# Six of nine token blocks taken as three pairs, gate and value from seven products of sums of quarters

## The chip, the core and the metric

The kernel runs on one core of a Trainium2 chip. The metric is device time in microseconds (us). Of the core's engines, TensorE (PE) multiplies matrices into banks of PSUM, VectorE (DVE) and ScalarE (ACT) do elementwise work, and SyncE (SP) issues most DMAs.

## The reference

Attention in chunks of 64 tokens, then a feed-forward layer with a gate. B = H = 8, S = 576, D = 64, all in float32:

```python
scores = scale * np.matmul(q_c, k_c.transpose(0, 1, 2, 4, 3))   # per chunk of 64
scores = scores - np.max(scores, axis=-1, keepdims=True)
attn = np.exp(scores)
attn = attn / (np.sum(attn, axis=-1, keepdims=True) + 1e-09)
out = np.matmul(attn, v_c)
...
x = np.ascontiguousarray(attn_out.transpose(0, 2, 1, 3)).reshape(B * S, H * D)   # 4608 x 512
g = x @ w_gate                                                   # 512 x 1536
silu = g * (1.0 / (1.0 + np.exp(-g)))
val = x @ w_val
return (silu * val @ w_out)                                      # 1536 x 512
```

## The kernel before

The 4608 tokens are 9 blocks of 512 (4 tiles of 128). A float32 operand is split into an upper and a lower half (`split`: a cast on ACT, a subtraction on DVE), and a product is three matmuls: lower by upper, upper by lower, upper by upper. The hidden dimension of 1536 is taken in 12 steps `f` of 128. In each step the gate and the value of a block are 12 matmuls each, of 128x128 by 128x512 (4 slices of the 512 inputs by 3), into a bank of `ps_gv`, which has two (line 416). `silu` on ACT reads the gate's bank, `times` on DVE multiplies by the value's bank, `parts` splits the result h into hh (ACT) and hl (DVE), and `project` does 12 matmuls against the step's output weights into four banks that stay open over the 12 steps (lines 460 to 462). `lag` issues the projection one step late.

The work runs in stages:

- an opening, written out as a string of operations: attention of blocks 0 and 1, and step 0;
- a **weight loop** over f = 1 to 10. The weights come as pairs of 32-bit words and are put together by `Up` (gate and value weights of step f + 1) and `Out` (output weights of step f) with scale, shift, below, power, weigh and join; then `upper` and `lower` make the halves `w` (128 x 2 x 1024). Each pass does gate and value of blocks 0 and 1 and the projection of block 0. The h of block 1 is written to DRAM (`put_off`);
- step 11, then a **late loop**: 12 projections of block 1, from h read back (`prepare`), beside block 2's softmax;
- blocks 2 to 8 one by one (`block`). Beside the steps of a block the next one's attention is done (`scores` behind step 1, `exponents` in step 3, `normalize`, `turn`, `values`, `ready`).

The order on PE, ACT and DVE is that in which the code is written, and on SP too up to `loading.__exit__` (line 746); behind it SP's order is chosen by the framework. All weights stay on chip, tiles `w0` to `w11` and `wo0` to `wo11`; out weights are split anew in each block (`out_weights`, pool `wp` of two buffers). Softmax of a block sits in `s_sb`, what `turn` makes of it in `turned`, and x in `xh0`, `xl0`, `xh1`, `xl1`.

## Time and profile before

| | |
|---|---|
| three runs | 952.35 us median (951.77 to 952.48) |
| the profiled execution | 952.15 us, of which the profile's span is 950.4 |
| instructions in it | 14625 |
| granted TensorE clock, mean | 1.0 |
| DMA | 63.85 MB, 67 GB/s mean; 50.33 MB read from and 12.58 MB written to device memory |
| DMAs of `raw<-in_wgv` (SP), 1024 KB | 11, 7.0 us median from issue to landing |
| DMAs of `out<-o_sb` (SP), 256 KB | 35, 2.3 us |
| DMAs of `h<-h` (ACT), 256 KB | 12, 2.0 us |
| DMAs of `h_in<-h` (SP), 512 KB | 6, 3.5 us |

A row of a group reads: line, engine, operation, written tile and read tile, shape, count, then busy time in all, mean of one in ns, the engine's idle time just ahead of these instructions, and what ended it. A row of the timeline reads: start and length in us, engine, line, operation, tiles, shapes, count, and in square brackets the wait ahead of it and who ended it. A row of who waited for whom ends with the wait in all, the count and the longest. A row of the windows has the stretch, then for each engine its busy share with the count of instructions, the granted clock, the DMA engines' busy share and the rate in GB/s.

### The profile page before, as it was taken

Reading aid. Unit: us, or ns where it says so; the run is one execution under the profiler, and the core shown is the slowest. Engines: PE = TensorE matmul, PEld = TensorE weight load, DVE = VectorE, ACT = ScalarE, POOL = GpSimd, SP = SyncE. Lnnn points to the kernel's source line nnn. Section 1 sums busy time; section 2 is a strip of 40 time slices with the busy share of each in tenths; the row PEclk is TensorE's granted clock in tenths of the full one; section 3 lists DMA queues with packets and bytes.
Section 4 is the critical chain, followed back from the end, with each engine's and each line's share of the span. In section 5 each row is a group of like instructions: output and inputs, shape, how many; then the busy total and the mean of one; then the engine's idle time right before and its main releaser. Section 6 shows DMA issues by size and latency. Waiting matters only on the chain.

```text
span 950.4 us, 14625 instructions
## 1 busy us (share of the span) xinstructions
PE 940.5 (99%) x6299; PEld 778.6 (82%) x6299; DVE 480.4 (51%) x792; ACT 336.3 (35%) x540; POOL 7.0 (1%) x14
## 2 busy tenths in 40 slices
PE   7999999999999999999999999999999999999998
PEld 6888888888888888888888888888888888888886
DVE  7966666574475336632574337533663256432222
ACT  4745444354332333133323233233423342332222
POOL 1100000000000000000000000000000000000000
PEclk9999999999999999999999999999999999999999
DMA  9614332443300230022102030023002210000001
GB/s 363 228 54 155 155 111 99 156 167 112 89 1 1 89 87 3 1 90 67 23 0 90 1 90 1 5 84 90 1 1 89 67 23 1 1 16 29 1 1 44
DMA packets 43936, 63.85 MB, mean 67 GB/s; under 512 B 27488, under 2 KB 27744, under 8 KB 42464
## 3 DMA queue, kind: packets, MB, share of 16 engines
q1 hardware_dynamic: 42144, 59.78, 18.3%
q10 hardware_dynamic: 1728, 3.15, 0.9%
q8 instruction: 49, 0.80, 0.3%
q14 instruction: 15, 0.12, 0.0%
HBM read 50.33 MB, written 12.58 MB: 66 GB/s over the span
## 4 chain that ended last, share of the span: by engine, by line
PE 97%; DMA 2%; SPq 0%; issue 0%; ACT 0%; DVE 0%
PE ps_gv L416 62%; PE ps_o L460 10%; PE ps_o L462 10%; PE ps_o L461 10%; PE ps_a L228 2%; DMA qk_t<-in_qk 2%; PE ps_a L306 1%; PE ps_a L406 1%; PE ps_a L585 0%; PE ps_a L392 0%; DMA out<-o_sb 0%; PE pt L392 0%; SPq L200 0%; SPq L154 0%; SPq L345 0%
## 5 line engine op out<-in xcount | busy, mean ns | idle before, releaser
L416 PE MATMUL ps_gv<-xh,w 128*128 128x512 f32 x1728 | 531.0, 389 | 0.0
L416 PEld LDWEIGHTS ps_gv<-xh,w 128*128 128x128 f32 x1728 | 324.3, 188 | 67.4 <-ACT xh L535 0.2
L416 PE MATMUL ps_gv<-xl,w 128*128 128x512 f32 x864 | 336.1, 391 | 0.0
L441 DVE SCALAR_TENSOR_TENSOR h<-ps_gv,h 128x512 f32<-128x512 f32 x108 | 74.6, 691 | 365.1 <-PE ps_gv L416 357.8
L416 PEld LDWEIGHTS ps_gv<-xl,w 128*128 128x128 f32 x864 | 162.1, 188 | 34.6 <-issue 0.4
L434 ACT ACTIVATE h<-ps_gv 128x512 f32<-128x512 f32 x108 | 64.6, 598 | 313.0 <-PE ps_gv L416 313.0
L460 PE MATMUL ps_o<-woh,hl 128*128 128x512 f32 x432 | 168.4, 390 | 0.0
L461 PE MATMUL ps_o<-wol,hh 128*128 128x512 f32 x432 | 168.1, 389 | 0.0
L462 PE MATMUL ps_o<-woh,hh 128*128 128x512 f32 x432 | 168.1, 389 | 0.0
L64 ACT CAST hh<-h 128x512 fp32r<-128x512 f32 x96 | 59.6, 620 | 182.7 <-DVE h L441 182.7
L461 PEld LDWEIGHTS ps_o<-wol,hh 128*128 128x128 f32 x432 | 81.1, 188 | 16.9
L460 PEld LDWEIGHTS ps_o<-woh,hl 128*128 128x128 f32 x432 | 81.1, 188 | 16.9
L462 PEld LDWEIGHTS ps_o<-woh,hh 128*128 128x128 f32 x432 | 81.1, 188 | 16.8
L293 DVE STREAM_TRANSPOSE turned<-s_sb 32x256 f32<-32x256 f32 x192 | 83.7, 436 | 2.7
L65 DVE TENSOR_TENSOR wol<-wo,woh 128x512 fp32r<-128x512 f32 x108 | 73.8, 684 | 12.7 <-ACT woh L64 12.6
L65 DVE TENSOR_TENSOR hl<-h,hh 128x512 fp32r<-128x512 f32 x96 | 66.4, 692 | 18.1 <-ACT hh L64 11.1
L64 ACT CAST woh<-wo 128x512 fp32r<-128x512 f32 x108 | 66.1, 612 | 15.9 <-DVE wo L102 15.9
L228 PEld LDWEIGHTS ps_a<-qk_t 64*64 64x64 f32 x1152 | 18.0, 135 | 5.4 <-issue 3.4
L228 PE MATMUL ps_a<-qk_t 64*64 64x64 f32 x1152 | 19.8, 220 | 1.6 <-DMA qk_t<-in_qk 1.6
L99 DVE TENSOR_TENSOR t<-t 128x1024 bf16<-128x1024 bf16 (+1 forms) x13 | 8.5, 650 | 22.1 <-ACT t L91 21.9
L475 ACT ACTIVATE o_sb<-ps_o 128x512 f32<-128x512 f32 (+1 forms) x36 | 18.6, 593 | 2.2 <-PE ps_o L462 2.0
L136 ACT CAST w<-t 128x1024 fp32r<-128x1024 f32 x11 | 11.6, 1054 | 16.7 <-DVE t L102 16.7
(70 smaller groups left out, 409.1 us busy)
## 6 DMA issues: line engine op xcount, KB each, us to landing
raw<-in_wgv SPq DMA_DIRECT2D x11, 1024.0 KB, 7.0
qk_t<-in_qk SPq DMA_DIRECT2D x10, 1024.0 KB, 7.5
out<-o_sb SPq DMA_DIRECT2D x35, 256.0 KB, 2.3
qk_t<-in_qk SPq DMA_DIRECT2D x16, 512.0 KB, 4.0
raw<-in_wo SPq DMA_DIRECT2D x6, 1024.0 KB, 4.9
v_t<-in_v SPq DMA_DIRECT2D x28, 128.0 KB, 2.7
h<-h ACTq DMA_DIRECT2D x12, 256.0 KB, 2.0
h_in<-h SPq DMA_DIRECT2D x6, 512.0 KB, 3.5
```

The source lines that it names most:

```text
L64: nc.scalar.copy(out=hi, in_=src)
L65: (engine or nc.vector).tensor_tensor(out=lo, in0=src, in1=hi.bitcast(F32), op=ALU.subtract)
L136: nc.scalar.copy(out=self.w[:, 0], in_=self.t)
L228: nc.tensor.matmul(ps[h][j * C:(j + 1) * C, i, u // 2, :], part[:, us:us + C], part[:, M * P + us:M * P + us + C], start=not more or first ...
L293: nc.vector.transpose(out=self.turned[to:to + 32, p:p + 2, j, :, 32 * (i % 2):32 * (i % 2) + 32], in_=src[32 * i:32 * i + 32, :, o // 2, 3 ...
L416: nc.tensor.matmul(ps, w, x, start=first and (k, i) == which[0], stop=last and (k, i) == which[-1])
L434: nc.scalar.activation(h, pg, AF.Silu, scale=2.0 ** -8)
L441: nc.vector.scalar_tensor_tensor(out=h, in0=pv, scalar=2.0 ** -8, in1=h, op0=ALU.mult, op1=ALU.mult)
L460: nc.tensor.matmul(o, hl[:, ts], woh, start=f == 0, stop=False)
L461: nc.tensor.matmul(o, hh[:, ts], wol, start=False, stop=False)
L462: nc.tensor.matmul(o, hh[:, ts], woh, start=False, stop=f == NF - 1)
L475: nc.scalar.activation(o_sb[:, m], o[:, m], AF.Copy, scale=2.0 ** -8)
```

## The change

Blocks 3 to 8 are taken as pairs (3, 4), (5, 6) and (7, 8). A pair's x is a 2 x 2 matrix of quarters (block by half of the 512 inputs), and so is a step's weight (half of the inputs by gate or value). `gated_pair` makes gate and value of both blocks from seven products of 6 matmuls (`seventh`), of quarters and of sums of quarters (`FACTORS`, `x0` to `x6`), in place of 4 x 12 matmuls. Three products are copied out of PSUM by ACT and three are added to by DVE. The projection of the first block lags as before, but a tile of it is put between the products (`turn_of`); the second block's h is kept on chip in the tiles of `xh0` to `xl1`, and its 12 projections follow in `second_steps`.

The factors on the weights' side (`w`, and the sums of its quarters, `ts`, split into `th` by `Quarters`) are not all kept on chip. In the weight loop each pass adds three subtractions, a cast and a subtraction for the sums and saves them to DRAM (`save`); steps 0 and 1, which the loop doesn't reach, are caught up by `redo` in block 2. The halves `w` are saved in block 2 (`save_w`), the split output weights in the weight loop (`save_o`). From then on they are loaded: 1024 KB of `w` and 1024 KB of sums per step of a pair (`load_weights`, two steps ahead, two buffers of each), and 512 KB of output weights per projection (`out_again`, three buffers), from block 1's late projections on. The output weights' raw tiles become four in turn. While block 2 runs alone, the attention of blocks 3 and 4 is done beside it, with its order by step in `behind`; later pairs' attention lies beside the steps of the pair ahead (`behind`, `later`).

```diff
-    wp = ctx.enter_context(tc.tile_pool(name="wp", bufs=2))
+    wp = ctx.enter_context(tc.tile_pool(name="wp", bufs=3))
...
+    Q = NK // 2 * P
+    class Quarters:
+        def __init__(self, f):
+            self.f = f
+        def again(self):
+            self.both = const.tile([P, 2, 4 * Q], F32, name="th", tag="th")
+            w = w_both[self.f].bitcast(F32)
+            nc.vector.tensor_tensor(out=self.both[:, 0], in0=w[:, 0], in1=w[:, 1], op=ALU.add)
+            return self.both[:, 0]
+        def sums(self, t):
+            self.s = s = const.tile([P, 4, Q], F32, name="ts", tag="ts")
+            t = t.rearrange("p (i q) -> p i q", q=Q)
+            nc.vector.tensor_tensor(out=s[:, 0:2], in0=t[:, 2:4], in1=t[:, 0:3:2], op=ALU.subtract)
+            nc.vector.tensor_tensor(out=s[:, 2], in0=t[:, 3], in1=s[:, 0], op=ALU.subtract)
+            nc.vector.tensor_tensor(out=s[:, 3], in0=t[:, 1], in1=s[:, 2], op=ALU.subtract)
+        def upper(self):
+            self.halves = const.tile([P, 2, 4 * Q], F32R, name="th", tag="th")
+            self.s = self.s.rearrange("p i q -> p (i q)")
+            nc.scalar.copy(out=self.halves[:, 0], in_=self.s)
+        def lower(self):
+            nc.vector.tensor_tensor(out=self.halves[:, 1], in0=self.s, in1=self.halves[:, 0].bitcast(F32), op=ALU.subtract)
+        def save(self):
+            kept_t[self.f] = store.tile([P, 2, 4 * Q], F32, name=f"t{self.f}")
+            nc.sync.dma_start(out=kept_t[self.f], in_=self.halves.bitcast(F32))
+    kept_w, kept_t, kept_o = {}, {}, {}
+    def save_w(f):
+        kept_w[f] = store.tile([P, 2, 4 * Q], F32, name=f"w{f}")
+        nc.sync.dma_start(out=kept_w[f], in_=w_both[f].bitcast(F32))
...
-            wo_raw.append(const.tile([P, DM], F32, name=f"wo{self.f}"))
+            wo_raw.append(const.tile([P, DM], F32, name="wo", tag=f"wo{self.f % 4}"))
...
-    def out_weights(f, engine=None):
-        woh = wp.tile([P, DM], F32R, name="woh")
-        wol = wp.tile([P, DM], F32R, name="wol")
-        split(wo_raw[f], woh, wol, engine)
-        return woh, wol
+    def out_weights(f):
+        both = wp.tile([P, 2, DM], F32R, name="both", tag="wo")
+        split(wo_raw[f], both[:, 0], both[:, 1])
+        kept_o[f] = store.tile([P, 2, DM], F32, name=f"o{f}")
+        out_now[f] = both
+        return both[:, 0], both[:, 1]
...
+    out_now = {}
+    def save_o(f):
+        nc.sync.dma_start(out=kept_o[f], in_=out_now[f].bitcast(F32))
+    def out_again(f):
+        both = wp.tile([P, 2, DM], F32R, name="both", tag="wo")
+        nc.sync.dma_start(out=both.bitcast(F32), in_=kept_o[f])
...
+    quarters = None
     for f in range(1, NF - 1):
         w, o = up[f + 1], down[f]
         if f + 2 < NF:
             up[f + 2].load()
+        save_o(f - 1)
         down[f + 1].load()
+        if quarters:
+            quarters.save()
+        quarters = Quarters(f + 1)
         h0 = gate(a0, f)
...
         w.lower()
+        quarters.sums(w.t)
         o.weigh()
         o.join()
         if f + 2 < NF:
             up[f + 2].scale()
         down[f + 1].scale()
+        quarters.upper()
         wo_f = out_weights(f)
         lag(p0, wo_f)
+        quarters.lower()
         h1 = gate(a1, f)
         pv1 = value(a1, f)
...
-        return p, out_weights(f)
+        return p, out_again(f)
...
     put.append(prepare(1))
+    save_o(f - 1)
+    quarters.save()
+    save_o(f)
     pv1 = value(a1, f)
     times(h1, pv1)
     put_off(h1)
...
+    class Pair:
+        def __init__(self, b, turned):
+            self.a = [Attn(b)]
+            self.b, self.turned, self.x = b + 1, turned, {}
+        def second(self):
+            self.a.append(Attn(self.b, const, "th", self.turned))
+            return self.a[1]
+        def quarter(self, i, j):
+            return self.a[i].s[:, 2 * j:2 * j + 2].rearrange("p n c h k -> p (n c h k)")
+        def halves(self, i, src):
+            x = self.x[i] = const.tile([P, 2, NK // 2, N], F32R, name="x", tag=f"w{i}")
+            split(src, *(x[:, j].rearrange("p k n -> p (k n)") for j in range(2)))
+        def x0(self):
+            self.halves(0, self.quarter(0, 0))
+        def x1(self):
+            self.sum = ld.tile([P, NK // 2 * N], F32, name="sum", tag="qk_t")
+            nc.vector.tensor_tensor(out=self.sum, in0=self.quarter(1, 0), in1=self.quarter(1, 1), op=ALU.add)
+            self.halves(1, self.sum)
+        def x2(self):
+            a11, a21 = self.quarter(0, 0), self.quarter(1, 0)
+            nc.vector.tensor_tensor(out=a21, in0=a11, in1=a21, op=ALU.subtract)
+            nc.vector.tensor_tensor(out=a11, in0=self.sum, in1=a11, op=ALU.subtract)
+            self.halves(2, a11)
+        def x3(self):
+            self.halves(3, self.quarter(0, 1))
+        def x4(self):
+            self.halves(4, self.quarter(1, 0))
+        def x5(self):
+            a11, a12 = self.quarter(0, 0), self.quarter(0, 1)
+            nc.vector.tensor_tensor(out=a12, in0=a12, in1=a11, op=ALU.subtract)
+            self.halves(5, a12)
+        def x6(self):
+            self.halves(6, self.quarter(1, 1))
...
+    FACTORS = (0, 0), (1, 0), (1, 2), (0, 1), (1, 1), (0, 3), (1, 3)
+    loaded = {}
+    def load_weights(f):
+        tags = ("w7", "w8") if f % 2 == 0 else ("w9", "w10")
+        loaded[f] = []
+        for kept, tag in zip((kept_w, kept_t), tags):
+            t = const.tile([P, 2, 4 * Q], F32R, name="factors", tag=tag)
+            nc.sync.dma_start(out=t.bitcast(F32), in_=kept[f])
+            loaded[f].append(t)
+    def seventh(ps, pair, f, i, first):
+        which, q = FACTORS[i]
+        w = loaded[f][which].rearrange("p h (i k m) -> p h i k m", i=4, m=P)[:, :, q]
+        x = pair.x[i]
+        for k in range(NK // 2):
+            for n, (u, v) in enumerate(((0, 1), (1, 0), (0, 0))):
+                nc.tensor.matmul(ps, w[:, u, k], x[:, v, k], start=first and k == 0 and n == 0,
+                                 stop=k == NK // 2 - 1 and n == 2, skip_group_check=True)
...
+        ps1 = ps_a.tile([P, N], F32, name="ps_a", tag="ps_a")
+        ps2 = ps_gv.tile([P, N], F32, name="ps_gv")
+        ps3 = ps_gv.tile([P, N], F32, name="ps_gv")
+        h = hp.tile([P, N], F32, name="h")
+        v1 = const.tile([P, N], F32, name="v1", tag=f"wo{f % 2}")
+        v2 = const.tile([P, N], F32, name="v2", tag=f"wo{2 + f % 2}")
+        seventh(ps1, pair, f, 0, True)
+        nc.scalar.copy(out=h, in_=ps1)
+        seventh(ps2, pair, f, 1, True)
+        nc.scalar.copy(out=v2, in_=ps2)
+        turn_of(0)
+        seventh(ps1, pair, f, 2, False)
+        nc.scalar.copy(out=v1, in_=ps1)
+        seventh(ps3, pair, f, 3, True)
+        add(h, ps3)
+        nc.scalar.activation(h, h, AF.Silu, scale=2.0 ** -8)
+        turn_of(1)
+        seventh(ps1, pair, f, 4, False)
+        add(v2, ps1)
+        seventh(ps2, pair, f, 5, False)
+        add(v1, ps2)
+        times(h, v1)
+        turn_of(2)
+        seventh(ps1, pair, f, 6, False)
+        nc.scalar.activation(h2, ps1, AF.Silu, scale=2.0 ** -8)
+        times(h2, v2)
+        turn_of(3)
+        return h
...
+    def both_steps(pair, behind, nothing=lambda: None):
+        kept = []
         for f in range(NF):
-            wo_f = []
-            def between():
-                middle.get(f, lambda: None)()
-                wo_f.extend(out_weights(f))
-            h = gated(a, f)
-            between()
-            lag(parts(a, f, h), wo_f)
-            behind.get(f, lambda: None)()
-        return nxt
-    a = nxt
-    for b in range(2, NB):
-        a = block(a, b)
+            if f % 2 == 0:
+                tag = ("xh0", "xl0", "xh1", "xl1")[f // 2 % 4]
+                kept.append(xs.tile([P, 2, N], F32, name="h2", tag=tag))
+            wo_f = out_again(f)
+            h = gated_pair(pair, f, kept[-1][:, f % 2])
+            p = parts(pair.a[0], f, h)
+            behind.get(f, nothing)()
+            lag(p, wo_f)
+            if not (pair.last and f + 2 >= NF):
+                load_weights((f + 2) % NF)
+        pair.kept = kept
...
+        put = [(parts(pair.a[1], f, pair.kept[f // 2][:, f % 2]), out_again(f)) for f in range(2)]
+        for f in range(NF):
+            lag(*put.pop(0))
+            behind.get(f, nothing)()
+            if f + 2 < NF:
+                put.append((parts(pair.a[1], f + 2, pair.kept[(f + 2) // 2][:, f % 2]), out_again(f + 2)))
...
+    a, pair = nxt, Pair(3, "w2")
+    c = pair.a[0]
+    first = {0: Quarters(0), 1: Quarters(1)}
+    def redo(f):
+        q = first[f]
+        q.sums(q.again())
+        q.upper()
+        q.lower()
+        q.save()
+    behind = {0: lambda: (redo(0), scores(c, False)), 1: lambda: (softmax_and_turn(c, 0), redo(1)),
+              2: lambda: (softmax_and_turn(c, 1), softmax_and_turn(c, 2)),
+              3: lambda: (softmax_and_turn(c, 3), load_v(c)), 4: lambda: values(c), 5: lambda: scores(pair.second(), False),
+              6: lambda: softmax_and_turn(pair.a[1], 0),
+              7: lambda: (softmax_and_turn(pair.a[1], 1), softmax_and_turn(pair.a[1], 2)),
+              8: lambda: (softmax_and_turn(pair.a[1], 3), load_v(pair.a[1]), load_weights(0)),
+              9: lambda: (values(pair.a[1]), pair.x0(), pair.x1()), 10: lambda: (pair.x2(), pair.x3()),
+              11: lambda: (pair.x4(), pair.x5(), load_weights(1), pair.x6())}
+    for f in range(NF):
+        save_w(f)
+        h = gated(a, f)
+        wo_f = out_again(f)
+        lag(parts(a, f, h), wo_f)
+        behind[f]()
+    for b in range(3, NB, 2):
+        pair.last = b + 2 == NB
+        behind, later = {}, {}
+        if not pair.last:
+            n = Pair(b + 2, "w11")
+            c = n.a[0]
+            behind = {1: lambda: scores(c), 2: lambda: softmax_and_turn(c, 0),
+                      3: lambda: (softmax_and_turn(c, 1), softmax_and_turn(c, 2)), 4: lambda: softmax_and_turn(c, 3),
+                      6: lambda: scores(n.second()), 7: lambda: softmax_and_turn(n.a[1], 0),
+                      8: lambda: (softmax_and_turn(n.a[1], 1), softmax_and_turn(n.a[1], 2)),
+                      9: lambda: (softmax_and_turn(n.a[1], 3), load_v(c))}
+            later = {0: lambda: values(c), 1: lambda: (load_v(n.a[1]), n.x0()), 3: lambda: (values(n.a[1]), n.x1()),
+                     4: lambda: n.x2(), 6: lambda: n.x3(), 7: lambda: n.x4(), 8: lambda: n.x5(), 10: lambda: n.x6()}
+        both_steps(pair, behind)
+        second_steps(pair, later)
+        if not pair.last:
+            pair = n
```

What moves is shown at three places. The first is **DVE in one pass of the weight loop**, from the power of the output weights (`o_sb<-wo`) through the weights' lower half (`w<-t,w`) to the product h of the next pass; `ts` and `th` are the sums and their halves, `both` holds the output weights' halves (before: `wol`). With the change:

```order
L94 TENSOR_SCALAR o_sb<-wo 128x512
L142 TENSOR_TENSOR w<-t,w 128x1024
L165 TENSOR_TENSOR ts<-t 128x512
L166 TENSOR_TENSOR ts<-t,ts 128x256
L167 TENSOR_TENSOR ts<-t,ts 128x256
L99 TENSOR_TENSOR o_sb<-o_sb 128x512
L102 TENSOR_TENSOR wo<-wo,o_sb 128x512
L65 TENSOR_TENSOR both<-wo,both 128x512
L175 TENSOR_TENSOR th<-ts,th 128x1024
L497 SCALAR_TENSOR_TENSOR h<-ps_gv,h 128x512
```

Before:

```order
L94 TENSOR_SCALAR o_sb<-wo_712 128x512
L141 TENSOR_TENSOR w<-t,w 128x1024
L99 TENSOR_TENSOR o_sb<-o_sb 128x512
L102 TENSOR_TENSOR wo_712<-wo_712,o_sb 128x512
L65 TENSOR_TENSOR wol<-wo_712,woh 128x512
L441 SCALAR_TENSOR_TENSOR h<-ps_gv,h 128x512
```

Three subtractions now stand between the weights' lower half and the join of the output weights (L102), and a fourth behind their split.

The second is **SP where the late projections of block 1 begin**: `both<-o_…` is a load of output weights, `out` and `v_t` are block 0's outputs and block 2's v, `h_in` block 1's h, and `o_…<-both` and `t_…<-th` are saves of output weights and of sums. With the change:

```order
L477 DMA both<-o_711 128x1024
L532 DMA out<-o_sb 128x512 x4
L827 DMA v_t<-in_v 64x512
L823 DMA v_t<-in_v 128x512
L780 DMA h_in<-h_1182 128x1024
L827 DMA v_t<-in_v 64x512
L823 DMA v_t<-in_v 128x512
L827 DMA v_t<-in_v 64x512 x2
L477 DMA both<-o_783 128x1024
L473 DMA o_1778<-both 128x1024
L179 DMA t_2018<-th 128x2048
L473 DMA o_1909<-both 128x1024
```

Before:

```order
L476 DMA out<-o_sb 128x512 x4
L760 DMA v_t<-in_v 64x512 x2
L716 DMA h_in<-h_1141 128x1024
L756 DMA v_t<-in_v 128x512 x2
L760 DMA v_t<-in_v 64x512 x2
L716 DMA h_in<-h_1342 128x1024
```

The second load of output weights now stands behind four outputs, six loads of v and one of h, and three saves come behind it.

The third is **ACT in steps 1 and 2 of block 2**, from the silu of step 1 (`h<-ps_gv`) to that of step 2, with the exp of the next block's scores (`s_sb`) between. With the change:

```order
L490 ACTIVATE h<-ps_gv 128x512
L64 CAST hh<-h 128x512
L294 ACT_TABLE_LOAD
L294 ACTIVATE s_sb<-s_sb 128x2048
L172 CAST th<-ts 128x1024
L490 ACT_TABLE_LOAD
L490 ACTIVATE h<-ps_gv 128x512
L64 CAST hh<-h 128x512
```

Before, the exp stood in step 3, and its neighbours were these:

```order
L434 ACTIVATE h<-ps_gv 128x512
L249 ACT_TABLE_LOAD
L249 ACTIVATE s_sb<-s_sb 128x2048
L64 CAST woh<-wo_873 128x512
L64 CAST hh<-h 128x512
L434 ACT_TABLE_LOAD
L434 ACTIVATE h<-ps_gv 128x512
```

The cast of the output weights is gone; between exp and the next step's silu there now stands the cast of the sums of step 1 of the weights (`th<-ts`), which follows DVE.

More of the change, by code (lines that the diff above doesn't have):

```diff
@@ L452, in parts, with project @@
         return a, f, hh, hl
-    def project(parts, wo_f):
+    def project(parts, wo_f, which=range(T)):
         (a, f, hh, hl), (woh, wol) = parts, wo_f
@@ L457, in project @@
             a.o = [ps_o.tile([P, DM], F32, name="ps_o") for _ in range(T)]
-        for t in range(T):
+        for t in which:
             ts, o = slice(t * P, (t + 1) * P), a.o[t]
@@ L525, in attn_then_gated_ffn @@
         for c in range(2):
[L526 removed]
+            pool, tag = (ld, "v_t") if a is a0 else (wp, "wo")
             odd = pool.tile([P, 2 * T, C], F32, name="v_t", tag=tag)
@@ new lines, in load_v, with values @@
+    def load_v(a):
+        a.v = [a.load_v_crossed(p, "v_t" if p < 2 else "qk_t") for p in range(NP)]
+    def values(a):
+        a.columns_crossed(a.v[:2], 0, 2, ps_gv, "ps_gv")
+        a.columns_crossed(a.v[2:], 2, 2)
+    class Pair:
[31 more added lines that the diff above has]
+            self.halves(6, self.quarter(1, 1))
@@ new lines, in add, with gated_pair, turn_of @@
+    def add(t, ps):
+        nc.vector.tensor_tensor(out=t, in0=t, in1=ps, op=ALU.add)
+    def gated_pair(pair, f, h2, lagging=True):
+        def turn_of(t):
+            if lagging and pending:
+                project(*pending[0], which=[t])
+                if t == T - 1:
+                    pending.pop()
+        ps1 = ps_a.tile([P, N], F32, name="ps_a", tag="ps_a")
[26 more added lines that the diff above has]
+        return h
```

51 lines of the change are left out of this document (25 added, 26 removed).

## The prediction

> **What bounds the kernel now.** I read the page's busy times and clock first, then the chain that ended last, then who waited on PE (TensorE's matmuls), then the timeline of one pass.
>
> ```profile
> PE 940.5 (99%) x6299; PEld 778.6 (82%) x6299; DVE 480.4 (51%) x792; ACT 336.3 (35%) x540; POOL 7.0 (1%) x14
> PEclk9999999999999999999999999999999999999999
> PE 97%; DMA 2%; SPq 0%; issue 0%; ACT 0%; DVE 0%
> 77.41 10.88 PE ps_gv L416 x48
> 298.79 5.44 PE ps_gv L416 x24
> PE ps_a L585 <- DVE tops L578: 2.1, 2, 1.1
> PE unread L60 <- POOL ident masks.py:199: 1.4, 1, 1.4
> ```
>
> PE is the chain. 24 matmuls in 5.44 us are 0.2267 us each, 48 in 10.88 the same: they follow one another without a gap, and after the opening PE waits for nobody. So a matmul removed is worth 0.2267 us, and any wait put on PE costs its whole length, since nothing stands in reserve.
>
> **What is removed.** A step of a pair of blocks has 7 products of 6 matmuls, 42; two single blocks have 48.
>
> ```profile
> L416 PE MATMUL ps_gv<-xh,w 128*128 128x512 f32 x1728 | 531.0, 389 | 0.0
> L416 PE MATMUL ps_gv<-xl,w 128*128 128x512 f32 x864 | 336.1, 391 | 0.0
> ```
>
> Of these 2592, six go in each of 12 steps of 3 pairs: 216, and 216 x 0.2267 = **49.0 us**. Every other group on PE keeps its count. The rest of the sum is what PE newly waits for.
>
> **A: the weight loop, 10 passes.** DVE now subtracts quarters between the weights' lower half and the last steps on the output weights.
>
> ```profile
> 91.09 0.69 DVE L65 TENSOR_TENSOR hl<-h,hh 128x512 fp32r<-128x512 f32 x1 [1.04 <-ACT hh L64]
> 91.70 0.42 DVE L94 TENSOR_SCALAR o_sb<-wo 128x512 int16<-128x512 int16 x1
> 92.04 1.22 DVE L141 TENSOR_TENSOR w<-t,w 128x1024 fp32r<-128x1024 f32 x1
> 93.17 0.42 DVE L99 TENSOR_TENSOR o_sb<-o_sb 128x512 bf16<-128x512 bf16 x1
> 93.63 0.69 DVE L102 TENSOR_TENSOR wo<-wo,o_sb 128x512 f32<-128x512 f32 x1
> 94.35 0.62 ACT L64 CAST woh<-wo 128x512 fp32r<-128x512 f32 x1 [1.68 <-DVE wo L102]
> 94.88 0.59 ACT L434 ACTIVATE h<-ps_gv 128x512 f32<-128x512 f32 x1
> 96.28 0.39 PE L416 MATMUL ps_gv<-xl,w 128*128 128x512 f32 x1
> 100.89 0.69 DVE L99 TENSOR_TENSOR t<-t 128x1024 bf16<-128x1024 bf16 x1 [2.33 <-ACT t L91]
> 89.49 1.05 ACT L136 CAST w<-t 128x1024 fp32r<-128x1024 f32 x1 [1.67 <-DVE t L102]
> ```
>
> The chain is DVE L102, then ACT's cast, then silu, which frees the bank that PE writes from 96.28. Silu ends at 95.47: 0.8 us of slack. Starts show that a 512-wide subtraction takes DVE 0.61 us, a 1024-wide one 1.13, so a 256-wide one about 0.35, an estimate; the three new ones take 1.3 us and overdraw the slack by 0.5 to 0.6. The next pass doesn't win it back: its hl comes from the weights' cast, that from DVE, that from ACT's L91, that from the next gate on PE, so the ring moves along: 10 x 0.55 = 5.5 us. The new cast of the sums (1.05, as L136) hides beside DVE's L99 and L102. The sums sit in one buffer, whose save must have landed before the next cast; in every other pass it is issued behind a 1024 KB load.
>
> ```profile
> raw<-in_wgv SPq DMA_DIRECT2D x11, 1024.0 KB, 7.0
> 107.00:108.00 1.00, 1.00 (x6) 0.84 (x5) 0.88 (x2) 0.11 (x2) 0.00 (x0) 1.00 1.00 426
> ```
>
> At 426 GB/s a second 1024 KB ends some 7 us after its issue, about 0.4 us late, 4 times: 1.5. A: **7 us** (0 if silu's slack is larger than I read; 13 with each save 2 us late).
>
> **B: the late projections of block 1.** Their output weights now come from DRAM, and SP takes its queue in order: the second load stands behind four outputs, six loads of v and one of h.
>
> ```profile
> 193.75 1.89 SPq L476 DMA_DIRECT2D out<-o_sb  x4
> 199.64 1.11 SPq L760 DMA_DIRECT2D v_t<-in_v  x2
> 203.00:204.00 1.00, 1.00 (x6) 0.83 (x5) 1.00 (x2) 0.68 (x2) 0.00 (x0) 1.00 0.89 309
> 197.01 0.23 PE ps_o L460
> ```
>
> The v loads are issued until 200.75 and move data until 204; the casts that vanish from ACT bring this some 0.5 us forward. 512 KB behind it lands at about 204.8. PE begins project 0 at 197.0 and, after 12 matmuls, wants project 1 at 199.7: 5 us. The third load waits for the saves of passes 10 and 11 (512 + 1024 + 512 KB, 4.9 us at 426 GB/s), and lands near 210.8, where project 2 could begin at 207.5: 3.3 us. Then loads of 3.5 us (h_in's median on the page) fit into the 5.4 us that three buffers give. B: **8.5 us**, between 3 (one load's latency alone) and 12.
>
> **C: block 2, alone, prepares a pair of blocks.** Its worst place is step 1.
>
> ```profile
> 254.03 0.69 DVE L244 TENSOR_TENSOR s_sb<-ps_a,top 128x512 f32<-128x512 f32 x1
> 261.43 1.28 ACT L249 ACT_TABLE_LOAD   x1
> 262.72 1.92 ACT L249 ACTIVATE s_sb<-s_sb 128x2048 f32<-128x2048 f32 x1
> 266.39 2.28 DVE L254 TENSOR_REDUCE z<-s_sb 128x32 f32<-128x2048 f32 x1
> 269.31 2.29 DVE L265 TENSOR_TENSOR s_sb<-s_sb,z 128x2048 f32<-128x2048 f32 x1
> 273.69 3.57 DVE L293 STREAM_TRANSPOSE turned<-s_sb 32x256 f32<-32x256 f32 x8
> 248.72 1.07 ACT L236 COPY s_sb<-ps_a 128x512 f32<-128x512 f32 x2 [2.42 <-PE ps_a L228]
> ```
>
> ACT's queue there: hh, table, exp, cast of weight 1's sums, table, silu of step 2. That cast needs DVE, which first does the sum and the scaling of the softmax. From the end of value 1: scores' subtraction still running 0.4, times to hh 1.4, table and exp 3.2 (5.0); sum to scaling 5.2 (10.2); adding the halves 1.13 and 1.3 of sums (12.6); cast 1.05, table 1.28, silu 0.6: 15.7. PE meanwhile has project, gate, value, project, 4 x 2.72 = 10.9, and then needs the bank: 4.9 us. In step 0 the same cast stands ahead of the two copies that free the scores' banks: 1.3. Steps 2 and 3 turn 16 pieces each (7.15 by the row of 8, and 2.0 for times, cast and hl): 19.0 us to the times of step 4, against 16.3 of PE's six groups: 2.7 before the values. The same once, for the second block: 1.7. At the first step of the pair three casts of quarters stand ahead of the copy that product 2 waits for: 1.8. C: **12.5 us** (7 to 16: the order leaves 4.9 no cover).
>
> **D: the joint steps.** Their own dependences close: copies and additions (0.6 to 0.7 us each) run beside the next product (1.36 us). Where an exp is queued, ACT reaches the copy of product 0 at 0.7 + 1.28 + 1.92 + 0.6 = 4.5 us, while PE has two products and a quarter of a projection, 3.4: 1.1 lost, four times; scores cost 0.3 more than now, four times. The 2 MB of factors for two steps on have a whole step of 12.2 us, with 7 needed. D: **5.5 us** (2 to 10).
>
> **E: the second block's projections.** The first lacks cover: hl of step 11 is ready 1.5 us after the last product (silu, times and hl, each 0.6 to 0.7, less the last projection), three times; x2's four DVE operations of 1.13 stand between two hl, 2.0 twice; v loads ahead of a weight load, 0.5 twice. E: **9.5 us** (4 to 13).
>
> **The sum.** Against the profiled execution's own 952.15 (span 950.4 and 1.75 around; 0.2 below the median): 952.15 - 49.0 + 7 + 8.5 + 12.5 + 5.5 + 9.5 = **946 us**. All lower ends give 952.15 - 49 + 16 = 919, all upper ends 952.15 - 49 + 64 = 967.
>
> **The rivals.**
>
> *Half of the waits have cover that I didn't see.* For it: each is a difference of long chains, and an end misread by 1 us removes several. Only the two that follow from a queue's order, B and C's step 1, are out of doubt. 21 us instead of 43: 924.
>
> *The saves bind the weight loop: slower.* Two passes now move 8.9 MB (decimal): 2 weights, 1 raw output load, 4 saves of 1024 KB, 2 of 512, 2 of h.
>
> ```profile
> h<-h ACTq DMA_DIRECT2D x12, 256.0 KB, 2.0
> ```
>
> This is the nearest row of a write to DRAM; none shows a long one. The 3.7 MB of the others take 8.7 us at 426 GB/s; 19.6 of the two passes' 28.3 us are left for 5.2 MB. Below 268 GB/s for saves PE waits for the buffer; from 247 it eats the gain; at 200 the passes cost 33 us more: 979.
>
> *The clock falls after a gap.* In this trace it stays at full, but PE's longest wait is 1.4 us. B and C open three gaps of 5, 3.3 and 4.9. If the 15 matmuls behind each took twice 0.2267, that is 3.4 each: 956. The Trainium skill (TensorE: Matmul & The Clock Gate, section The HAM clock gate) says that one idle window of about 3.4 us drops the array to half clock and that a busy one restores it. By that rule the gaps of 5 and 4.9 would often be hit, and the sum would be about 953; no run here shows it yet.
>
> *Whole gain:* all waits covered, 905. *The change doesn't do what it says:* factors come too late and each step waits; at 150 GB/s 2.6 MB need 17.5 us, 5 more than a step, 36 times: 1130. The rows at 426 speak against it.
>
> **How the numbers follow.** The forecast, 946 with a range of its own of 938 to 954, has 0.50; half covered 0.24; clock 0.10; saves 0.10; whole gain 0.03; factors late 0.03. The range of 922 to 962 leaves out the saves, the late factors, the whole gain and a little of the second. Beyond 0.2%, about what a measurement here can tell from no change, means below 950.4 or above 954.3. Faster: 0.40 of the forecast, 0.24, 0.03: 0.67. Same: 0.07 and 0.03 of the clock: 0.10. Slower: 0.03, 0.07, 0.10, 0.03: 0.23.
>
> **What would show it.** Matmuls into ps_gv and ps_a by pairs: 1512, at 0.2267 apart. PE's waits: for ACT's silu in the weight loop every pass, for the output weights' loads twice near 200 us, for silu once by 5 us in block 2's step 1, for hl at the head of each second block. The weight loop's pass should be 14.1 to 14.4 us, not 13.6. A pass of 13.6, or waits in B or C below half of mine, would show the second rival; ACT's cast of the sums waiting for a DMA the third; a granted clock below 1.0 the fourth. I am wrong most simply if waits that I call independent share a cause and vanish together.

## The result: slower by 2.9%

The changed kernel takes **980.21 us** (median of 4 runs, 977.0 to 980.86), the kernel before 952.27 (4 runs); the ratio is 1.0287, 95% interval 1.0265 to 1.031. The prediction was 946, in a range of 922 to 962, so the sign was wrong. The profiled execution has a span of 978.1 us, 27.7 above that of before.

From the page, busy times and clock, then the two kinds of products of the pairs:

```profile
PE 915.6 (94%) x6083; PEld 746.8 (76%) x6083; DVE 550.2 (56%) x863; ACT 367.7 (38%) x561; POOL 6.1 (1%) x14
PEclk9999999998998999999999999999999899999999
L952 PE MATMUL ps_a<-x,factors 128*128 128x512 f32 x864 | 220.4, 390 | 5.1 <-ACT h L973 5.1
L952 PE MATMUL ps_gv<-x,factors 128*128 128x512 f32 x648 | 164.8, 390 | 0.0
```

864 + 648 = 1512 products stand where 1728 stood: the 216 matmuls went as forecast. But PE, busy for 99% before, stands still for 62.5 us of the span (9.9 before), and its clock falls below full. Who PE waited for (total, times, longest):

```profile
PE ps_gv L461 <- ACT h L490: 18.1, 11, 4.9
PE ps_o L516 <- DMA both<-o: 14.4, 4, 6.8
PE ps_o L516 <- DVE hl L65: 5.4, 4, 1.3
PE ps_a L952 <- ACT h L973: 5.1, 5, 1.8
PE ps_a L351 <- DMA v_t<-in_v: 3.1, 4, 1.4
```

PE's first gate matmul of a step divides both traces into the same stages. Step 11 of block 1 begins at 188.55 us before and 206.82 us with the change, step 0 of block 2 at 231.00 and 259.51, its step 11 at 325.42 and 372.06. Each stage against the prediction:

| stage | forecast | measured |
|---|---|---|
| to step 11 (weight loop), A | +7 | +18.3 |
| late projections, B | +8.5 | +10.2 |
| block 2, C without its last 1.8 | +10.7 | +18.1, less 4.2 for block 4's scores and values, which moved here: +13.9 |
| the pairs, beside the -49.0 and the 4.2 that left them: D, E and C's 1.8 | +16.8 | +34.3 |

18.3 + 10.2 + 13.9 + 34.3 - 49.0 = 27.7. The waits cost more than their length. 13.2 us of PE's work is lost to the clock, in seven stretches that cost 1.6 to 2.4 us each. And at full clock each wait costs some 0.3 us of refill: the last matmul ahead of it ends 0.39 us after its start and the first behind it starts 0.34 us ahead of the next, where in a row both are 0.23.

### The profile page after: what moved, and what is told of

The parts are those of the page before. It is cut to its first block, busy times and chain, and to the rows that moved or that the text cites. A ratio compares the mean times of both kernels' runs of the same rounds, so it can differ in the third digit from the quotient of the medians.

```text
span 978.1 us, 14802 instructions
## 1 busy us (share of the span) xinstructions
PE 915.6 (94%) x6083; PEld 746.8 (76%) x6083; DVE 550.2 (56%) x863; ACT 367.7 (38%) x561; POOL 6.1 (1%) x14
## 3 DMA queue, kind: packets, MB, share of 16 engines
q10 hardware_dynamic: 1728, 3.15, 0.9%
## 4 chain that ended last, share of the span: by engine, by line
PE 62%; ACT 5%; DVE 5%; DMA 4%; issue 3%; SPq 1%; DVEq 0%; ACTq 0%
PE ps_a L952 20%; PE ps_gv L952 14%; PE ps_o L516 7%; PE ps_o L517 7%; PE ps_o L518 7%; PE ps_gv L461 4%; DMA both<-o 2%; DVE turned L338 1%; PE ps_a L273 1%; ACT s_sb L294 1%; DMA v_t<-in_v 1%; DVE hl L65 1%; ACT hh L64 1%; SPq L255 1%; ACT x L64 1%
## 5 line engine op out<-in xcount | busy, mean ns | idle before, releaser
L952 PE MATMUL ps_a<-x,factors 128*128 128x512 f32 x864 | 220.4, 390 | 5.1 <-ACT h L973 5.1
L516 PE MATMUL ps_o<-both,hl 128*128 128x512 f32 x432 | 173.1, 401 | 22.7 <-DMA both<-o 14.4
L952 PEld LDWEIGHTS ps_a<-x,factors 128*128 128x128 f32 x864 | 161.5, 188 | 40.6 <-ACT h L973 7.2
L461 PE MATMUL ps_gv<-xh,w 128*128 128x512 f32 x576 | 180.2, 397 | 0.0
L517 PE MATMUL ps_o<-both,hh 128*128 128x512 f32 x432 | 170.8, 395 | 0.0
L518 PE MATMUL ps_o<-both,hh 128*128 128x512 f32 x432 | 170.6, 395 | 0.0
L952 PE MATMUL ps_gv<-x,factors 128*128 128x512 f32 x648 | 164.8, 390 | 0.0
L952 PEld LDWEIGHTS ps_gv<-x,factors 128*128 128x128 f32 x648 | 121.3, 188 | 26.5 <-issue 1.5
L461 PE MATMUL ps_gv<-xl,w 128*128 128x512 f32 x288 | 114.5, 404 | 19.9 <-ACT h L490 18.1
L461 PEld LDWEIGHTS ps_gv<-xh,w 128*128 128x128 f32 x576 | 110.8, 192 | 23.4 <-ACT xh L591 0.2
L518 PEld LDWEIGHTS ps_o<-both,hh 128*128 128x128 f32 x432 | 82.7, 191 | 17.8
L517 PEld LDWEIGHTS ps_o<-both,hh 128*128 128x128 f32 x432 | 83.0, 192 | 16.9
```

Source lines behind the costliest of these rows:

```text
L461: nc.tensor.matmul(ps, w, x, start=first and (k, i) == which[0], stop=last and (k, i) == which[-1])
L516: nc.tensor.matmul(o, hl[:, ts], woh, start=f == 0, stop=False)
L517: nc.tensor.matmul(o, hh[:, ts], wol, start=False, stop=False)
L518: nc.tensor.matmul(o, hh[:, ts], woh, start=False, stop=f == NF - 1)
L952: nc.tensor.matmul(ps, w[:, u, k], x[:, v, k], start=first and k == 0 and n == 0, stop=k == NK // 2 - 1 and n == 2, skip_group_check=True)
```

## Experiments

All but the last change the changed kernel, and are held against its 980.2 us. Times are medians of 4 to 12 runs; b2 and the last have one run each.

### The weight loop: place, traffic or path?

The passes alternate: 14.5 us, and 16.2 to 16.5 where output weights are loaded too (one short pass takes 16.1, most of its 1.6 more at half clock). A long one in the timeline of the changed kernel (start, length, [wait, who ended it]):

```profile
76.44 0.38 SPq L224 DMA_DIRECT2D raw<-in_wo  x1
76.92 0.42 SPq L179 DMA_DIRECT2D t<-th  x1
77.39 0.42 SPq L121 DMA_DIRECT2D raw<-in_wgv  x1
81.91 0.32 SPq L185 DMA_DIRECT2D w<-w  x1
85.59 1.04 ACT L172 CAST th<-ts 128x1024 fp32r<-128x1024 f32 x1 [1.91 <-DMA t<-th]
86.55 0.61 ACT L64 CAST both<-wo 128x512 fp32r<-128x512 f32 x1
87.06 0.59 ACT L490 ACTIVATE h<-ps_gv 128x512 f32<-128x512 f32 x1
87.71 0.53 PE L461 MATMUL ps_gv<-xl,w 128*128 128x512 f32 x1 [2.61 <-ACT h L490]
```

Three transfers of 1024 KB start within 1 us; the cast of the sums waits for its buffer's save, and silu stands two places behind it on ACT. (The save of `w`, written in block 2, was issued here, as the prediction's sum of traffic had it.)

**Save first (a1).** `quarters.save()` moves ahead of the pass's two loads.

> In the weight loop the save of the sums is issued ahead of the two weight loads of the pass instead of behind them. Theory 'the save lands late because it is queued behind a load': the passes that now take 16.1 to 16.5 us fall to the 14.5 us of the short ones, about 1.7 us in each of five, so the loop is 8 to 9 us shorter and the kernel takes about 971 us; PE's waits of 2.3 to 2.6 us for silu shrink to 0.6. Rival 'the DMA engines are full in the loop': the load that is now behind comes late instead, the long passes stay at 16 us and the time within 2 us of 980.

Measured: **987.61 us**. ACT's waits for the save vanish, and 15.2 and 12.3 us of waits for the two loads (5.4 and 8.6 before) come in: the rival's outcome, with the time 7.4 us above the changed kernel's, where the rival said within 2.

**No saves of `w` in the loop (a3).**

```diff
-        nc.sync.dma_start(out=kept_w[f], in_=w_both[f].bitcast(F32))
+        nc.scalar.dma_start(out=kept_w[f], in_=w_both[f].bitcast(F32))
```

> The twelve 1024 KB saves of the weights' halves are issued by ACT's queue in block 2, a step each, instead of by SyncE's in the weight loop; the order of everything else is as written. Theory 'the long passes of the weight loop are bound by DMA traffic, to which these saves add': with a third of the traffic gone, the passes that load output weights fall from 16.1 to 16.5 us to the 14.5 of the others, the waits of ACT's scaling and cast for a DMA go, and the kernel takes 968 to 972 us. Rival 'it is the wait for the one buffer of sums, whatever the traffic': the long passes keep 16 us and the time is within 3 us of 980, or above where block 2 pays for the saves.

Measured: **982.26 us**, long passes as long as before.

**The path (a2).**

```diff
-        quarters.sums(w.t)
         o.weigh()
         o.join()
+        quarters.sums(w.t)
...
-        quarters.upper()
         wo_f = out_weights(f)
         lag(p0, wo_f)
-        quarters.lower()
         h1 = gate(a1, f)
+        quarters.upper()
+        quarters.lower()
```

> In each pass of the weight loop the sums of the quarters are taken behind the join of the output weights, and their cast stands behind silu of block 1 instead of ahead of it. Theory 'both the 0.6 us of the short passes and the 2.5 us of the long ones reach PE through silu, by way of the cast of the sums and of the join': with both off silu's path the passes return to 13.6 us, PE's waits for silu in the loop go, and the kernel takes 962 to 965 us. Rival 'the loop is bound by its ring or by the DMA': the passes stay above 14.4 us, another wait takes the place, and the time stays above 972.

Measured: **965.32 us**, 14.9 less; six passes take 84.1 us (14.0 each). The same 120 us of the loop, by windows (PE's busy time and matmuls, clock, DMA share, GB/s), in the changed kernel, in a3 and in a2:

```profile
60.00:180.00 120.00, 109.51 (x467) 0.99 0.75 277
```

```profile
60.00:180.00 120.00, 110.50 (x465) 0.97 0.58 209
```

```profile
60.00:180.00 120.00, 117.94 (x517) 1.00 0.79 304
```

A quarter less traffic won nothing, and the most traffic goes with the most work of PE. Neither the save's place in SyncE's queue nor the traffic as such bound the loop; the cast's place in ACT's queue did. What a2 leaves, 0.4 to 0.7 us every other pass, is `times` behind the cast's subtraction on DVE.

### The late projections: queue or buffer?

**v by another queue (b2).** The loads of block 2's v go from `nc.sync` to `nc.gpsimd`.

> The loads of block 2's v are issued by the GpSimd queue instead of SyncE's; nothing else moves. Theory 'buffer': the second late load of output weights waits until the first late projection has freed the only free buffer of three, since the other two hold output weights 10 and 11, whose saves come later; so it is still issued at the end of that projection (near 218.0 us), PE still waits 6 to 7 us, and the time stays within 2 us of 980. Rival 'queue', which is the prediction's: the load goes out some 4 us sooner, PE's wait falls to 3 us or less, and the kernel takes 974 to 976 us.

Measured: 978.65 us. The timeline of that run:

```profile
212.51 0.33 SPq L780 DMA_DIRECT2D h_in<-h  x1
216.08 0.33 SPq L477 DMA_DIRECT2D both<-o  x1
222.41 0.77 PE L516 MATMUL ps_o<-both,hl 128*128 128x512 f32 x1 [6.36 <-DMA both<-o]
```

SyncE's queue is empty from 212.8 on, and still the load waits until project 0 is done: the buffer theory.

**Saves ahead (b1).**

```diff
     lag(p0, wo_f)
+    save_o(f - 1)
     nxt.less_top(nxt.products([nxt.load_qk(2, 2, const, "turned")]), 2)
+    quarters.save()
     h1 = gate(a1, f)
     put = [prepare(0)]
     lag(None, None)
+    save_o(f)
     put.append(prepare(1))
-    save_o(f - 1)
-    quarters.save()
-    save_o(f)
```

> The saves of output weights 10 and 11 and of the last sums stand ahead of the late projections that they now follow, so that all three buffers are free in turn. Theory 'buffer': the second load of output weights no longer waits for the first projection; PE's waits of 6.8 and 1.6 us go, the granted clock's dip behind them too (0.83 in those 20 us), and the kernel takes 969 to 972 us. Rival 'the saves themselves fill the DMA engines there': the loads stand behind 2 MB of saves in the same stretch and PE still waits 4 us or more; 976 us or more.

Measured: **973.62 us**, 6.6 less; 1.6 us are left for the load and 1.9 behind DVE's softmax, so the size was less than I expected.

### Block 2: order or room?

**The cast behind silu (c1).** `redo` is split: sums behind the scores, `first[0].upper()` and `first[1].upper()` behind silu of steps 1 and 2, the rest behind the steps.

> In block 2 the casts of the sums of steps 0 and 1 stand behind the next step's silu, and the scores' copies ahead of the sums. Theory 'PE waits in steps 0 and 1 because ACT's queue holds silu and the copies behind a cast that waits for DVE': the waits of 1.8 and 4.9 us go, and with them the granted clock's dips behind them (0.91 and 0.83 in those 20 us); block 2 is 9 to 12 us shorter and the kernel takes 968 to 971 us. Rival 'DVE is the bound there': its work is the same, the turns and with them the values come later, PE waits there instead, and the time is 975 us or more.

Measured: 978.25 us, the rival: the 1.8 and 4.9 us went, and 2.15, 0.66 and 3.17 us behind `times` (DVE) came.

**The sums in the late loop (c2).** The same work in steps 5 to 8 of `extra`.

> The sums for steps 0 and 1 of the weights are taken in the late loop (its steps 5 to 8) instead of in block 2. Theory 'DVE has no room for them beside block 2's softmax, but has room in the late loop': block 2's waits of 1.8 and 4.9 us and the clock's dips there (0.91 and 0.83) go, and only some 2 us come back in the late loop; the kernel takes 969 to 973 us. Rival 'the late loop has no room either, with 2.7 us of PE a step': waits of 5 us or more for hl there, 976 us or more.

Measured: **973.54 us**. Both waits went; 0.45 us for hl came in the late loop, and 1.5 us behind `times` (DVE) ahead of block 3's values, where the changed kernel had none. DVE beside block 2's softmax had no room; the late loop had.

### The pairs

**Exp and split inside the step (de1).**

```diff
         nc.scalar.copy(out=v1, in_=ps1)
+        middle()
...
         times(h, v1)
+        p = parts(pair.a[0], f, h)
```

`middle` holds the exp of steps 2 and 7.

> In the pairs the exp stands inside the step, behind the copy of the third product, instead of ahead of the next step's first copy; and the first block's h is split ahead of the second block's silu. Theory 'ACT's order makes these waits': the four waits of 0.8 us and the three of 1.3 us at the end of the joint steps go, each with some 0.3 us in which PE fills again; 6 to 8 us less, 972 to 974 us. Rival 'the exp inside the step delays silu and with it a product': waits of 1 us or more for h appear in those steps and the time is within 2 us of 980.

Measured: **974.81 us**; the four waits of 0.8 us are gone, the three of 1.3 are 0.3.

**The second steps.** The timeline of the changed kernel, and windows of it (PE's busy time and matmuls, clock, DMA share, GB/s):

```profile
551.66 1.64 SPq L255 DMA_DIRECT2D v_t<-in_v  x2
553.40 1.02 SPq L477 DMA_DIRECT2D both<-o  x2
557.74 0.47 PE L516 MATMUL ps_o<-both,hl 128*128 128x512 f32 x1 [1.98 <-DMA both<-o]
571.23 0.47 PE L516 MATMUL ps_o<-both,hl 128*128 128x512 f32 x1 [3.44 <-DMA both<-o]
```

```profile
548.00:551.00 3.00, 3.00 (x15) 1.00 0.70 167
551.00:554.00 3.00, 1.73 (x71) 1.00 0.56 124
565.00:571.20 6.20, 2.78 (x13) 1.00 1.03 412
```

The two waits differ. The load that ended the first was issued at 553.40, behind twelve loads of v and four outputs that SyncE issued from 542.3 on, while the DMA engines had room. The load that ended the second was issued at 563.86 and took 7.2 us to land, with the engines full.

**f1:** v by the GpSimd queue from block 3 on. **f2:** that, and the second block's `values` behind step 5 instead of 3.

> From block 3 on the loads of v are issued by the GpSimd queue instead of SyncE's. Theory 'SyncE's queue': it spends 0.55 to 0.8 us on each of some 18 small loads at the start of the second steps, and the output weights and the v that are wanted stand behind them; PE's waits there for v (3.1 us in all) and for output weights (1.98, 3.44 and 2.21 us) go, with the clock's dips at 560 to 580 and 760 to 780 us; the kernel takes 966 to 971 us. Rival 'the transfers are late by traffic or latency, whoever issues them': waits of 6 us or more in all remain and the time is 976 us or more.

> v by the GpSimd queue, as in the run of that alone (977.1 us), and the second block's values in the second steps taken behind step 5 instead of 3, with the quarters of x that follow them two steps on or one. Theory 'v is late because its buffers come free only when the first block's values are done, one step ahead': with two more steps of 2.7 us PE's waits for v in the second steps (6.3 us in all) go, the clock's dips with them, and the kernel takes 967 to 971 us. Rival 'traffic delays what is wanted there': 3 us or more of waits stay, for v or for output weights, and the time is 974 us or more.

Measured: 977.06 and 981.01 us. In f1 no wait for output weights is left there, and 6.3 us for v are; in f2 none for v, but 5.2 and 2.5 for output weights and up to 3.0 for hl. Each cure moved the wait. In f1 SyncE issues the load of the 1.98 us wait at 547.02, but the DMA engines are full (a share of 0.96 to 1.02 from 543 to 559 us, at 304 to 353 GB/s), and it lands at 557.52.

### Together

> The sums behind the join (a2), the early saves (b1), the sums of steps 0 and 1 in the late loop (c2) and the two moves inside the pairs' steps (de1) together. Alone they brought 14.9, 6.6, 6.7 and 5.4 us. Theory 'the waits are independent': 980.2 less 33.6 is 947 us, 944 to 950. Rival 'they share a cause, or one takes the room of another (the sums in the late loop stand where the early saves and loads must go)': less than three quarters of the sum, 955 us or more.

> The same five moves, and all loads of v from block 2 on by the GpSimd queue. If the waits are independent, what that queue brings alone comes on top: 9 to 14 us less than the five moves, 933 to 940 us, so that the pairs of seven products are faster than the kernel before. If issue order is not what makes the output weights late in the second steps, it stays at 944 us or above.

g1 takes **945.71 us**, g2 945.01 (ratios to the kernel before 0.9935, interval 0.9917 to 0.9953, and 0.9921, 0.9905 to 0.9936). The five moves add up: 34.5 against 33.6. The queue of v brings nothing on top.

Four more sought what is left. g3 and g4 have the later values and the last sums' save behind the late loads; h1 and h2 take 4 MB of the next pair's factors out of the second steps' start and put them, by ACT's queue, between later projections.

> The five moves (945.7 us alone), v of blocks 3 and on by the GpSimd queue, the second block's values two steps later, and the save of the last sums behind the first two late loads of output weights. If buffers and order make the waits that are left, those for v and for output weights in the second steps (10 us in all with the dips) and half of the 3.3 us in the late loop go: 932 to 937 us. If traffic makes them, 942 us or more.

> The same with v left on SyncE's queue. If the queue is what makes output weights late there, their waits of 4.4 and 1.8 us stay and the time is 939 us or more; if the two steps are enough for both, it is within 2 us of the kernel with v by the GpSimd queue.

> The five moves (945.7 us), and the factors of the next pair's steps 0 and 1 are loaded by ACT's queue in steps 5 and 8 of the second steps, instead of by SyncE's at the end of the joint steps. Theory 'traffic': without these 4 MB the v and the output weights of the first five second steps come in time; PE's waits there for them (1.9, 4.4, 1.6 and 1.8 us in the two pairs) shrink to 2 us in all and the dip goes, 934 to 939 us. Rival 'SyncE's issue of small loads': they stay above 7 us, 943 us or more.

> The same with v of blocks 3 and on by the GpSimd queue. Theory 'traffic': as the other within 3 us, or some 2 us better, as neither cause is left; 932 to 938 us. Rival 'v's buffers': the waits for v stay at 5 us or more, and the time at 942 us or more.

Measured: 949.71, 954.05, 954.47 and 948.32 us: all above g1. In g3 and g4 PE waits 4.3 to 6.0 us for output weights in each pair's second steps, and the save that moved makes a wait of 4.4 and 4.5 us at the late projections, where g1 has 1.8; in h1 and h2 the first pair's waits of before stay (4.9 us for output weights in h1, 3.9 for v in h2), and the 2 MB bursts make new ones of up to 4.4 us between projections of 2.7 us.

**h3:** as g3 with the save as in g1, and 2 MB of factors moved to the start of the next pair's step 0.

> The five moves, v of blocks 3 and on by the GpSimd queue, the second block's values two steps later (all as in g3, 949.7 us, where PE waited 5.9 and 4.3 us for output weights in the second steps), and the 2 MB of factors of the next pair's step 1 loaded at the start of its step 0, where a step has 12 us, by ACT's queue. Theory 'traffic': in the first six second steps some 2 MB less move ahead of the output weights, so both waits fall below 2 us, and the time to 937 to 942 us. Rival 'not traffic, but the place of these loads in the queue or their latency': both waits stay above 3 us and the time at 945 us or more.

Measured: **942.37 us** (6 runs, 939.52 to 946.35), ratio to the kernel before **0.9901** (0.988 to 0.9922), the best. Part of the 7.3 us that it gains on g3 is the save's: the wait at the late projections is 1.75 us again. Of the two waits one fell. The timeline has SyncE's rows ahead of the first wait, and PE's of both pairs:

```profile
509.84 1.85 SPq L532 DMA_DIRECT2D out<-o_sb  x4
511.79 1.49 SPq L245 DMA_DIRECT2D qk_t<-in_qk  x1
513.66 5.76 SPq L477 DMA_DIRECT2D both<-o  x3
525.26 0.76 PE L516 MATMUL ps_o<-both,hl 128*128 128x512 f32 x1 [6.18 <-DMA both<-o]
...
723.25 0.47 PE L516 MATMUL ps_o<-both,hl 128*128 128x512 f32 x1 [1.34 <-DMA both<-o]
```

In the second pair the wait went from 4.3 to 1.3 us with the 2 MB, which speaks for traffic. In the first it stayed (5.9 in g3), and there a 1024 KB load of a later block's q and k stands ahead of three loads of output weights; the second pair has none. The DMA engines are full there (0.99 from 513.6 to 525.2 us, at 328 GB/s). A kernel without that load was not run, so what it costs stays open.

### The clock, in the kernel before

```diff
+            for _ in range(AGAIN.get((a.b, f), 0)):
+                nc.vector.tensor_tensor(out=p[3], in0=h, in1=p[2].bitcast(F32), op=ALU.subtract)
             lag(p, wo_f)
```

> The kernel before, in which DVE subtracts the lower half of h again and again (12, 14, 15, 16, 18 and 20 times in step 0 of blocks 3 to 8; 14, 15, 14 and 15 times in steps 2, 4, 6 and 8 of block 8), so that PE has gaps of graded length with nothing else changed: by 0.61 us a subtraction and 6.1 us of cover some 1.2, 2.4, 3.1, 3.7, 4.9 and 6.1 us. Theory 'a gap lowers the granted clock for some us behind it, from a length between 2 and 3.4 us on, and the same length can go either way': behind gaps of 3.7 us and more the matmuls stand 0.43 us apart instead of 0.2267 for about 3 us, behind 1.2 never, behind 2.4 to 3.1 in some. Rival 'the dips in the changed kernel come from something else there, such as traffic': matmuls keep 0.2267 us apart behind every gap.

The subtractions took 0.72 us each, so the gaps were 2.9 to 8.7 us, and the shorter ones that I wanted are missing. The shortest:

```profile
350.22 0.77 PE L460 MATMUL ps_o<-woh,hl 128*128 128x512 f32 x1 [2.88 <-DVE hl L837]
350.78 0.63 PE L461 MATMUL ps_o<-wol,hh 128*128 128x512 f32 x1
351.21 0.63 PE L462 MATMUL ps_o<-woh,hh 128*128 128x512 f32 x1
...
353.30 0.39 PE L461 MATMUL ps_o<-wol,hh 128*128 128x512 f32 x1
353.54 0.40 PE L462 MATMUL ps_o<-woh,hh 128*128 128x512 f32 x1
```

Starts 0.43 us apart, then 0.24: half clock for 3 us. All ten gaps did this, at a cost of 1.5 to 3.1 us each. The kernel before has none of the changed kernel's loads and saves, so a gap alone is enough. 1031.18 us in one run: 52.8 of waits, 24 of clock, the rest the refills.

The length that counts is not that of the gap. In these traces the recorded clock changes only at the edges of steps of 3.41 us, and what decides is PE's idle time within one step. Windows of that length of the changed kernel, two at its gap of 2.61 us (85.10 to 87.71) and three at its gap of 2.45 us (117.69 to 120.14):

```profile
84.63:88.04 3.41, 0.80 (x4) 1.00 1.00 423
88.04:91.45 3.41, 3.41 (x10) 0.50 1.03 425
```

```profile
115.35:118.76 3.41, 2.34 (x11) 1.00 1.01 425
118.76:122.17 3.41, 2.03 (x9) 1.00 0.99 417
122.17:125.59 3.42, 3.42 (x17) 1.00 1.05 380
```

The first gap lies in one step, and the next step runs at half clock. An edge cuts the second in two, 1.07 and 1.38 us, and the clock stays. By PE's recorded idle time in the 19 traces other than the kernel before's: of the steps at full clock none of the 4999 with less than 1.58 us idle was followed by half clock, all 84 with 1.92 us or more were, and 23 of the 52 between. Full clock came back behind each of the 107 steps at half clock with less than 0.6 us idle, and behind none of the 61 others.

## Why the prediction was wrong, step by step

The forecast was 34 us too low: A by 11.3, B by 1.7, C by 3.2, D and E with the 1.8 by 17.5. 13.2 of this is the clock, which the sum put at nothing, and some 0.3 for each wait is the refill, which it left out.

- **-49.0:** right. 216 matmuls fewer, and a joint step runs at 12.2 us where nothing waits.
- **A, 7 us, was 18.3.** The path was right (a2): cast, silu, gate. The short passes' 0.6 us wait is the 0.5 to 0.6 of the text. Mis-sized was "about 0.4 us late, 4 times": the save was priced at 426 GB/s with one load ahead, and it shared the engines with two others, so it was 1.9 us late (put ahead of both in a1, it was in time and they were later). That is the "13 with each save 2 us late" of the bounds: the ten waits make 13.2 us. Refills add 3, the clock 1.7, and 0.5 was lost ahead of the loop.
- **B, 8.5 us, was 10.2.** A right size for a wrong reason, so luck: the waits were 6.8 and 1.6, and the clock added 1.6. "The second load stands behind four outputs, six loads of v and one of h" fell with b2: the load waited for a buffer, since two of the three held weights that were saved only later in the program.
- **C, 10.7 us, was 13.9.** Places and lengths were mostly right: 1.8, 4.9, none and 1.5 us measured for 1.3, 4.9, 2.7 and 1.7. The 2.7 ahead of block 3's values was covered by PE's waits in steps 0 and 1: with those gone 3.2 came there in c1 and 1.5 in c2. The clock added 4.1 in its two stretches, which the forecast left to a rival. That a cast merely stands at a bad place is refuted by c1: DVE had no room.
- **D and E with the 1.8, 16.8 us, were 34.3.** This is the largest miss. The waits for hl and the exp were about as forecast (1.3 for 1.5, 0.8 for 1.1); x2's 2.0 twice was 1.35 once. What failed is "v loads ahead of a weight load, 0.5 twice": 3.1 us of waits for v, 7.6 for output weights. The path was right and far too short: the loads of v and the outputs hold SyncE's queue for some 11 us in each of the first two pairs, and the loads that PE waits for 1.98 and 2.21 us are issued only behind them, at 553.40 and 758.28. Without v in that queue (f1) these waits go, but v's double, as the DMA engines are full. The transfers of the stretch were never added up: in the first pair's five second steps to x2, 13.6 us of PE, stand five loads of output weights, four outputs, a block's v, 1024 KB of q and k and 2 MB of factors, 7.9 MB, which take 18.5 us at the 426 GB/s of the prediction's row. The clock added 5.7.
- **The rivals.** "The clock falls after a gap" was given 0.10, as an alternative; it is no alternative but a charge on top of the waits, 13.2 us in all. "The saves bind the weight loop" gave 979, and 979 it nearly was. Its sign came too, the cast waiting for a DMA, four times 1.9 us; but the loop took 18.3 us more and not its 33, and with the cast off silu's path it ran at 14.0 us a pass with all saves in it (a2). "Half of the waits have cover" failed: nearly none had.

The Trainium skill (TensorE: Matmul & The Clock Gate, section The HAM clock gate) says that one idle window of about 3.4 us halves the clock. The half clock agrees, and the recorded clock does change in steps of 3.41 us; but a step needn't be idle throughout: 1.92 us of it were always enough in these traces. So gaps of 2.6 and 2.9 us did it, and others of 2.3 and 2.5, cut in two by an edge, didn't.

The change itself isn't lost: with five moves of order it beats the kernel before by 0.65%, and with h3's by 1%.

## What to carry to other kernels

A kernel in which one engine never waits has no reserve: count what each edit puts ahead of the instruction that frees that engine's bank, and charge each wait its length, 0.3 us of refill and, where some 1.9 us of idle time can fall in one step of 3.41 us, about 1.7 us of clock. A buffer is free when its last use *in program order* is done, so a save that is written late holds it. Before blaming traffic, take it away: here the loop was no faster with a quarter less, and faster with more. Before blaming a queue, look at when the wanted load was issued and how full the DMA engines were: emptying the queue filled them.

## What the runs showed that was not expected

- Gaps of 1.83 and 1.98 us (to 271.69 and 557.74 us in the changed kernel) were enough for half clock, each within one step of 3.41 us, where longer ones of 2.31 to 2.45 us were not.
- Loads wanted within some 10 us gained little from a second queue: in the first pair's second steps of h3 v's 128 and 64 KB pieces, by the GpSimd queue, landed in 7.2 and 7.5 us (medians), while the DMA engines were full.
